# Attention and a two-layer expert in one planned kernel: the order of the first batch's units, a planner that counts instruction transfers, and one operation less per weight block

## The chip, the cores and the metric

The kernel runs on one core of one Trainium2 chip. The metric is the device time of one execution in microseconds (us). Before the change three runs gave 985.59, 986.07 and 987.94 us; the median is 986.07 us. The engines are PE (TensorE matmuls), PEld (its weight loads), DVE (VectorE), ACT (ScalarE), POOL (GpSimd) and SP (SyncE, which here only issues DMAs).

## The reference

Inputs are q, k and v (float32) of 8 batches, 8 heads, 576 positions and 64 channels, and the weights w_in (512 x 2048) and w_out (2048 x 512), which arrive as float64. The output is float32.

```
q_d, k_d, v_d = means of q, k, v over groups of 4 positions        # 144 positions
out_up  = repeat(softmax(q_d k_d^T / 8) v_d, 4)                     # each pooled row serves 4 positions
out_loc = softmax over |i - j| < 4 of (q k^T / 8), times v          # a band of 7 positions
x = (out_up + out_loc), heads side by side                          # 4608 tokens x 512
h = x @ w_in;  g = h * clip(h + 3, 0, 6) / 6
out = g @ w_out
```

## The kernel before, in words

**Tiling.** A unit is two heads of one batch on 128 partitions, so a batch has 4 units, named (batch, unit) below. A unit's work: load q, k and v, pool them by 4, pooled scores (L427) and banded scores (L605 puts the mask there, L613 multiplies), two softmaxes (L457 to L475), transposes of the probabilities (L482, L622), pooled products (L561), banded products (L633), and an addition into x (L663). For batch 0, q and k are transposed by PE (L279). Tokens are cut into chunks: 512, 256, then 384 each. For each chunk, x is split into a high part (L127 or L129) and a low part (L814), and then come, for 16 blocks of 128 hidden channels, the first expert product (L887, 12 matmuls), the gate (L894 relu on ACT, L898 on DVE), the gated value's high and low part (L902, L906) and the second expert product (L930, 3 matmuls for each 128 tokens).

**Weights.** They come as 64-bit words. For each of the 32 blocks (wi0 to wi15, wo0 to wo15) the kernel makes float32 bits from the two halves of a word: ACT rescales the high half (L180 into a PSUM bank for 5 early blocks, L184 in place for 27) and takes the top 3 bits of the low half (L195); DVE shifts the high half by 3 (L189), puts the sign in by an or (L191), and DVE or POOL adds the low bits (L199). ACT then writes the rounded part (L204) and DVE or POOL the rest (L208). A block that uses a PSUM bank holds it until its L208 is done; the banks are those that L930 writes (o0, o1, o2) or attention uses (a0 to a2).

**Order.** A planner (`Plan.emit`, L1177) simulates the five engines with costs written in the code, picks on each engine the ready operation whose latest time is smallest, and writes all instructions out in that order; each engine runs its own in that order. Latest times come from due times: `need(b)` less `unit_time` for each unit that follows in its batch. `UNIT_T` is 1.5 us for batch 0. `SLOTS` says which PSUM bank or piece of memory an operation may take.

**Unread products.** Where the plan sees a gap on PE before the first L887, `busy(n)` (L956) puts in n matmuls of 512 columns whose result nobody reads (L963), one for each 0.22 us of the gap less 0.1.

Of the kernel before, what the change touches and what calls it, by code (L numbers as in the profile page):

```python
# [64 lines left out]
def tile_local_down_attention_moe(ctx, tc, q_all, k_all, v_all, _qk_loc, _v_loc, w_in, w_out, ident_d, _mask_d, out):  # L65
# [7 lines left out]
    nc = tc.nc  # L73
# [89 lines left out]
    def plan_weight(n, kind, f, after, gate):  # L163
# [22 lines left out]
        def bits(i):  # L186
            z, high = zf_t[key].bitcast(I32), words["high"]
            if i == 0:
                nc.vector.tensor_scalar(z, z if by_bank else high, 3, None, op0=ALU.logical_shift_left)  # L189
            else:  # L190
                nc.vector.scalar_tensor_tensor(  # L191
                    out=z, in0=high, scalar=-0x80000000, in1=z, op0=ALU.bitwise_and, op1=ALU.bitwise_or)

        def low():
            nc.scalar.activation(words["low"], words["low"].bitcast(U32), AF.Copy, scale=2.0 ** -29)  # L195

        def add(eng):
            z = zf_t[key].bitcast(I32)
            eng.tensor_tensor(z, z, words["low"], op=ALU.add)  # L199

# [12 lines left out]
        c = op("ACT", 0.68, low, [ld])  # L213
        if by_bank:
            b = op("DVE", 0.75, partial(bits, 1), [op("DVE", 0.66, partial(bits, 0), [a])])
            d = op("DVE", 0.72, partial(add, nc.vector), [b, c])
        else:
            b = op("DVE", 0.75, partial(bits, 1), [op("DVE", 0.5, partial(bits, 0), [a])], lock=True)
            d = op(on("add", 1.0), 0, add, [b, c], lock=True)
        e = w_hi[key] = op("ACT", 0.6, hi, [d])  # L220
# [18 lines left out]
    def plan_duo(b, d, masked):  # L239
# [14 lines left out]
        if b < BY_PE:  # L254
            for kind, t in (("q", q_all), ("k", k_all)):
# [16 lines left out]
                for g in range(3):  # L272
# [14 lines left out]
                    l = pieces_[g if step == 3 else 0]  # L287
                    a = early_user(op("PE", 0.33, tr, [l], take=[(PS, key), ("qkd" + k0, hk)], free=[rk], lag=LAGT))
                    evicts[kind].append(op(
# [11 lines left out]
    def plan_unit(b, d, u, row0, k0, kv, PS, duo, evicts, users, masked, early_user, due):  # L301
# [377 lines left out]
        if alone:  # L679
            sd = early_user(op("PE", 0.9, scores_d, [pooled["q"], pooled["k"]], take=[bk, pk, sk], lag=LAGT))  # L680
        else:
            sd = sl_op = op(
                "PE", 1.5, scores_all,
                turned["q"] + turned["k"] + [pooled["q"], pooled["k"]] + masked,
                take=[bk, pk, sk] + bks + [pl, sl], lag=LAGT)
        sd_ops.append(sd)
# [22 lines left out]
        if alone:  # L709
            sl_op = early_user(op("PE", 1.3, scores_n, turned["q"] + turned["k"] + masked, take=bks + [pl, sl], lag=LAGT))  # L710
        s_ops.append(sl_op)
# [24 lines left out]
        if alone:  # L736
            evs_d = []
            for g in range(2):
                bk = (PS, ("td", un, g))
                t = early_user(op(  # L740
                    "PE", 0.3, partial(trans_d, g), [softmax_d], take=[tk_d, bk], free=[pk],
                    lag=LAGT))
                evs_d.append(op(on("ev", 6 * QB), 0, lambda eng, g=g: evict_d(eng, g), [t], free=[bk]))
            bk = (PS, ("od", un))
            a = early_user(op("PE", 0.64, pv_d, evs_d + sums, take=[bk, ok], free=[tk_d, ("vd" + k0, un)], lag=LAGT))
            od = early_user(op("ACT", 0.29, mean, [a], free=[bk]))
# [8 lines left out]
        if alone:  # L755
            a = early_user(op("PE", 1.5, pv_n, [t] + lv + ([od] if b else []), take=bks + xbs, free=[tk, vk], lag=LAGT))
        else:
            a = op("PE", 1.4, pv_all, [t] + lv + turned_d + sums, take=bks + [ok] + xbs,
                   free=[tk, vk, tk_d, ("vd" + k0, un)], lag=LAGT)
            od = op("ACT", 0.29, mean, [a], free=[bks[0]])  # L760
            od = op("DVE", 0.31, mean_too, [od], free=[bks[1]])
# [108 lines left out]
    def plan_moe(n):  # L870
# [6 lines left out]
        for f in range(NF):  # L877
# [26 lines left out]
            def lo(eng, st=st, key=key):  # L904
# [4 lines left out]
            a = op("PE", 2.11 * share, gemm1, split_done[n] + [w_done["i", f]] + ([last1] if last1 else []),  # L909
                   take=[("h", key)], dl=dl)  # L910
            last1 = a
# [9 lines left out]
        for f in range(NF):  # L921
# [16 lines left out]
            if f == 0 or f == NF - 1:  # L938
                ops_ = []
                for m in range(parts):  # L940
                    take = [(f"o{m}", n)] if f == 0 else []
                    ops_.append(op("PE", cost, partial(g, m), after + prev[-1:], take=take, dl=dl))
                    prev.append(ops_[-1])
            else:
                def all_parts(g=g):
                    for m in range(parts):
                        g(m)

                ops_ = [op("PE", cost * parts, all_parts, after + prev[-1:], dl=dl)]
                prev += ops_  # L950
# [50 lines left out]
T0, TC, TF, LAG = 55.0, 82.0, 5.1, 2  # L1001
UNIT_T, EARLY, SLACK = (1.5, 30.0, 30.0), 0.7, 28.0
PRE, GATE = 4, 8
# [19 lines left out]
COST = {  # L1023
    "add": {"POOL": (1.5, 0.0), "DVE": (0.68, 0.0)},
    "lo": {"POOL": (1.32, 0.0), "DVE": (0.68, 0.0)},
# [9 lines left out]
}  # L1035
PEN = {"add": {"DVE": 0.0}, "lo": {"DVE": 0.0}, "pool4": {"POOL": -10.0}, "ev": {"DVE": 5.0}, "sum4": {"POOL": -10.0},
    "norm": {"DVE": 5.0}, "minus": {"DVE": 5.0}, "xhi": {"DVE": 1.0}, "xlo": {"POOL": 2.0}, "gl": {"POOL": 10.0}, "ob": {"DVE": 5.0}}
# [98 lines left out]
def dma(packets, size):  # L1136

    return packets * (5.0 + 0.0376 * size) / 16e3 if size > 256 else packets * (8.0 + 0.039 * size) / 16e3


class Plan:
# [4 lines left out]

    def op(self, eng, cost, fn, after=(), take=(), free=(), size=0, dl=None, lag=0.0, lock=False):
        o = Op(len(self.ops), eng, cost, fn, take, size, dl)

        o.lag, o.lock = lag, {True: ("DVE", "POOL"), False: ("POOL",)}[lock]  # L1150
# [34 lines left out]
    def emit(self, warm, last, busy):  # L1185
# [41 lines left out]
        def fits(o):  # L1227
# [12 lines left out]
            return got  # L1240

        n_done = 0
        while n_done < len(self.ops):
            for e in ready:
# [22 lines left out]
                o.start = t  # L1267
                order.append(o)
                engine_free[e] = t + o.cost
# [37 lines left out]
        self.total = t  # L1307
        at = None
        for o in order:
            if o.eng == "PE" and at is not None:  # L1310
                n = int((o.start - at - IDLE[1]) / IDLE[0])
                if n > 0:
                    busy(n)
            if o is last:
                at, warm = None, None
            elif o.eng == "PE" and at is not None:
                at = o.end
            elif o is warm:
                at = o.end + 1.0
            o.run()  # L1320


class Op:
    def __init__(self, n, eng, cost, fn, take, size, dl):
# [5 lines left out]
        self.deps, self.succ, self.frees = [], [], []  # L1330
        self.at = 0.0
        self.span = self.cost + 2.0 + size
# [75 lines left out]
```

## Time and profile before

| what | value |
|---|---|
| median of three runs | 986.07 us |
| the profiled execution, its own time | 984.95 us |
| its span (first to last instruction) | 983.2 us |
| mean granted TensorE clock | 0.979 of full |
| first L887 starts | 65.90 us |
| PE, DVE busy share of the span | 97%, 59% |

The profiled execution's own time is 1.75 us above its span, and 1.12 us below the median of the runs. Shares over the span hide the stages: up to the first L887 PE runs attention of batch 0 while q, k, v and weights arrive; after that it alternates the two expert products with the attention units of later batches. The windows view below gives each engine's busy time by such stretches.

### The profile page before, as it was taken

To read this page: it belongs to the slowest core of one execution; us is meant where nothing else is said; L and a number is where in the kernel's file an instruction comes from. 1 tells how busy PE (TensorE), PEld (TensorE's weight loads), DVE (VectorE), ACT (ScalarE), POOL (GpSimd) and SP (SyncE) were. 2 spreads that over 40 slices of the span, in tenths; PEclk is the share of its full clock that TensorE was granted. 3 is DMA by queue.
4 is the path that set the end of the run, shared out by engine and by line. 5 is a ranking of instruction groups with operands and counts; after the bars stand their busy time and mean duration, and the time that the engine had idled before them with its cause. 6 is when DMAs were issued, how large, how long until landed. Compare 5 with 4: busy or idle time off the path is not lost.

```text
span 983.2 us, 21408 instructions
## 1 busy us (share of the span) xinstructions
PE 949.3 (97%) x8379; PEld 822.0 (84%) x8379; DVE 580.3 (59%) x1135; ACT 323.2 (33%) x641; POOL 342.7 (35%) x465
## 2 busy tenths in 40 slices
PE   6898999999999999999999999999999999999996
PEld 4576878798888888888898988888998988998995
DVE  6577999677656666666636557666635553323222
ACT  3356655333222322323322322322322322322221
POOL 5547674437434234334304343433404320000000
PEclk9778999999999999999999999999999999999999
DMA  8955543426665464563524455453523430100101
GB/s 195 246 163 154 162 133 110 97 60 141 123 130 108 108 114 95 109 121 77 113 48 86 103 109 101 106 116 76 122 52 75 102 70 3 33 1 1 33 1 33
DMA packets 318277, 94.16 MB, mean 96 GB/s; under 512 B 263680, under 2 KB 304512, under 8 KB 318176
## 3 DMA queue, kind: packets, MB, share of 16 engines
q1 hardware_dynamic: 318176, 92.79, 42.8%
q8 instruction: 66, 1.08, 0.5%
q14 instruction: 35, 0.29, 0.1%
HBM read 70.12 MB, written 22.61 MB: 94 GB/s over the span
## 4 chain that ended last, share of the span: by engine, by line
PE 68%; SPq 3%; DVE 2%; DMA 1%; issue 1%; POOL 0%; ACT 0%; DVEq 0%; POOLq 0%
PE o L930 32%; PE h L887 31%; PE a L646 2%; PE a L585 1%; PE a L443 1%; PE a L550 1%; SPq L528 1%; SPq L314 1%; SPq L502 1%; DMA arena<-in_q_dram 0%; SPq L507 0%; DMA arena<-pl 0%; DVE arena L321 0%; DMA out_dram<-arena 0%; DVE arena L330 0%
## 5 line engine op out<-in xcount | busy, mean ns | idle before, releaser
L887 PE MATMUL h<-rounded,wi 128*128 128x384 f32 (+2 forms) x2240 | 432.0, 336 | 2.0 <-DVE arena L898 1.8
L930 PE MATMUL o<-wo,rounded 128*128 128x512 f32 x1680 | 429.8, 397 | 2.9 <-DVE wi L208 2.8
L887 PEld LDWEIGHTS h<-rounded,wi 128*128 128x128 f32 x2240 | 389.5, 188 | 25.0 <-DVE arena L898 2.9
L930 PEld LDWEIGHTS o<-wo,rounded 128*128 128x128 f32 x1680 | 309.7, 188 | 64.6 <-DVE wi L208 3.0
L898 DVE SCALAR_TENSOR_TENSOR arena<-arena,h 128x384 f32<-128x384 f32 (+2 forms) x192 | 105.3, 549 | 197.8 <-ACT arena L894 197.0
L894 ACT ACTIVATE arena<-h 128x384 f32<-128x384 f32 (+2 forms) x192 | 94.3, 491 | 377.0 <-PE h L887 368.8
L902 ACT CAST rounded<-arena 128x384 fp32r<-128x384 f32 (+2 forms) x192 | 98.1, 512 | 139.3 <-DVE arena L898 93.3
L906 DVE TENSOR_TENSOR rounded<-arena,rounded 128x384 fp32r<-128x384 f32 (+2 forms) x135 | 80.2, 595 | 98.8 <-PE o L930 75.7
L906 POOL TENSOR_TENSOR rounded<-arena,rounded 128x384 fp32r<-128x384 f32 (+2 forms) x57 | 62.0, 1088 | 211.8 <-PE o L930 85.8
L460 POOL TENSOR_TENSOR arena<-arena 128x640 f32<-128x640 f32 x24 | 30.3, 1262 | 75.3 <-DVE arena L457 44.7
L475 POOL TENSOR_TENSOR arena<-arena 128x432 f32<-128x432 f32 (+2 forms) x47 | 51.1, 1095 | 9.1 <-DVE arena L472 7.6
L463 ACT ACTIVATE arena<-arena 128x432 f32<-128x432 f32 (+2 forms) x58 | 35.6, 630 | 49.4 <-DVE arena L460 44.7
L321 DVE STREAM_TRANSPOSE arena<-arena 128x576 f32<-128x576 f32 x56 | 42.6, 762 | 6.4 <-DMA arena<-in_q_dram 5.0
L466 DVE TENSOR_REDUCE arena<-arena 128x3 f32<-128x432 f32 (+2 forms) x58 | 37.9, 672 | 5.8 <-ACT arena L463 5.7
L814 POOL TENSOR_TENSOR rounded<-arena,rounded 128x768 fp32r<-128x768 f32 (+1 forms) x9 | 13.3, 1477 | 71.3 <-DVE rounded L129 70.2
L814 POOL TENSOR_TENSOR rounded<-first,rounded 128x384 fp32r<-128x384 f32 (+1 forms) x7 | 9.9, 1411 | 69.0 <-DVE rounded L129 69.0
L457 DVE TENSOR_REDUCE arena<-a 128x2 f32<-128x288 f32 (+3 forms) x59 | 22.8, 406 | 11.1 <-PE a L443 4.0
L336 POOL TENSOR_TENSOR arena<-arena 128x144 f32<-128x144 f32 x46 | 27.2, 591 | 3.6
L535 DVE STREAM_TRANSPOSE arena<-arena 128x640 f32<-128x640 f32 x24 | 20.0, 834 | 13.5 <-DMA arena<-pl 13.3
L334 POOL TENSOR_TENSOR arena<-arena 128x144 f32<-128x144 f32 x23 | 11.4, 498 | 46.1 <-DMA arena<-in_k_dram 18.1
L330 DVE TENSOR_REDUCE arena<-arena 128x144 f32<-128x576 f32 x35 | 25.8, 741 | 2.4 <-PE a L443 0.9
L646 PEld LDWEIGHTS a<-arena 64*64 64x64 f32 x960 | 16.4, 134 | 11.4 <-issue 8.3
(193 smaller groups left out, 862.3 us busy)
## 6 DMA issues: line engine op xcount, KB each, us to landing
rawi<-in_w_in_dram SPq DMA_DIRECT2D x16, 512.0 KB
rawo<-in_w_out_dram SPq DMA_DIRECT2D x16, 512.0 KB
arena<-in_q_dram SPq DMA_DIRECT2D x112, 72.0 KB
arena<-in_k_dram SPq DMA_DIRECT2D x112, 72.0 KB
pl<-arena SPq DMA_DIRECT2D x24, 320.0 KB
arena<-pl SPq DMA_DIRECT2D x96, 80.0 KB
out_dram<-arena SPq DMA_DIRECT2D x96, 72.0 KB
arena<-in_v_dram SPq DMA_DIRECT2D x24, 256.0 KB
```

What stands on the lines that cost most here:

```text
L321: nc.vector.transpose(out=qk[kind], in_=st["raw", kind].rearrange("p j i -> p (j i)"))
L460: eng.tensor_tensor(out_, x, m.unsqueeze(2).broadcast_to(list(x.shape)), op=ALU.subtract)
L463: nc.scalar.activation(x, x, AF.Exp, scale=scale)
L466: nc.vector.tensor_reduce(out=s, in_=x, op=ALU.add, axis=AX.X)
L475: eng.tensor_tensor(x, x, s.unsqueeze(2).broadcast_to(list(x.shape)), op=ALU.mult)
L646: nc.tensor.matmul(st["px"][g][h * D:(h + 1) * D, at + lo:at + hi], st["v"][ks, jj, h * D:(h + 1) * D], st["pt"][ks, jj, half + lo:half + ...
L887: nc.tensor.matmul(ps, win[f][:, wt, kk * P:(kk + 1) * P], xs[part][:, kk], start=(i == 0), stop=(i == 3 * NK - 1))
L894: nc.scalar.activation(st["t"], st["ps"], AF.Relu, bias=3.0)
L898: nc.vector.scalar_tensor_tensor(out=t, in0=t, scalar=6.0, in1=st["ps"], op0=ALU.min, op1=ALU.mult)
L902: nc.scalar.copy(st["gh"], st["t"])
L906: eng.tensor_tensor(st["gl"], st["t"], st["gh"].bitcast(F32), op=ALU.subtract)
L930: nc.tensor.matmul(otile[n, m], gt[:, ms], wout[f][:, wt], start=(f == 0 and i == 0), stop=(f == NF - 1 and i == 2),)
```

## The change

- The first DVE step of a weight block becomes one `scalar_tensor_tensor`: shift by 3, then an or with the low bits. The addition (L199) is gone. The ACT step that makes the low bits gets a bias of -0.5, so that its rounding gives whole numbers 0 to 7. The first DVE step now waits for both ACT steps.
- `UNIT_T` for batch 0 goes from 1.5 to 4.0 us, which spreads the four units' due times.
- Each PE operation tells the planner how many matmuls it issues (`rec`). The new `Plan.fetch` counts them in blocks of 128 (93 for the first) and adds time to an operation that would run into the next block sooner than 4.5 us after the block before it was entered.
- Unread products are planned for 0.75 of a gap (0.375 of it before plan time 8).
- The planner's cost of a DMA with packets of up to 256 bytes changes from (8 + 0.039 size) to (1 + 0.1 size) per 16,000 packets.

```diff
@@ bits, low, add (weight blocks) @@
             if i == 0:
-                nc.vector.tensor_scalar(z, z if by_bank else high, 3, None, op0=ALU.logical_shift_left)
+                nc.vector.scalar_tensor_tensor(
+                    out=z, in0=z if by_bank else high, scalar=3, in1=words["low"],
+                    op0=ALU.logical_shift_left, op1=ALU.bitwise_or)
...
-            nc.scalar.activation(words["low"], words["low"].bitcast(U32), AF.Copy, scale=2.0 ** -29)
-
-        def add(eng):
-            z = zf_t[key].bitcast(I32)
-            eng.tensor_tensor(z, z, words["low"], op=ALU.add)
+
+            nc.scalar.activation(words["low"], words["low"].bitcast(U32), AF.Copy, scale=2.0 ** -29, bias=-0.5)
...
+        b = op("DVE", 0.75, partial(bits, 0), [a, c], lock=not by_bank)
+        d = op("DVE", 0.75, partial(bits, 1), [b], lock=not by_bank)
...
-UNIT_T, EARLY, SLACK = (1.5, 30.0, 30.0), 0.7, 28.0
+UNIT_T, EARLY, SLACK = (4.0, 30.0, 30.0), 0.7, 28.0
...
-IDLE = 0.22, 0.1
+IDLE = 0.22, 0.1, 0.75
+
+FETCH = 128, 93, 4.5
...
+    def fetch(self, o):
+
+        t = o.start
+        if self.idle is None and self.warm.start is not None:
+            self.idle = self.warm.start + 1.2
+        if o is self.last:
+            self.last = None
+        if self.last is not None and self.idle is not None:
+            gap = (t - self.idle - IDLE[1]) * (IDLE[2] if t > 8.0 else 0.5 * IDLE[2])
+            o.busy = max(0, int(gap / IDLE[0]))
+        for n, first, took in ((o.busy, self.idle or 0.0, IDLE[0] * o.busy), (o.rec, t, o.cost)):
+            at, done = first, 0
+            while n - done >= self.left:
+                at += took * self.left / n
+                done += self.left
+                stall = max(0.0, self.block + FETCH[2] - at)
+                at += stall
+                if n is o.rec and first == t:
+                    o.cost += stall
+                self.block, self.left = at, FETCH[0]
+            self.left -= n - done
+        self.idle = t + o.cost
```

The instructions stand in another order on every engine. PE has 36 unread products before the first expert product where it had 63, and all else that it computes is the same. In the order's rows a name such as o0_597 is a tile in bank o0, "x48" counts matmuls as written, of which the chip runs L613, L427, L633 and L561 (L608, L422, L628 and L556 after the change, 5 lines earlier) as two each.

PE, between the second and the fourth unit of batch 0. Before, the last transposes of q and k (L279) come early, and three units' banded scores stand close together:

```order
L427 MATMUL o0_243<-early_160,arena_65 64x144 x6
L279 MATMUL o1_257<-ident_72,rows_64 128x128 x3
L279 MATMUL o2_263<-ident_72,rows_64 128x128 x3
L279 MATMUL h0_268<-ident_72,rows_64 128x128 x3
L427 MATMUL a0_273<-early_160,arena_65 64x144 x6
L605 LDWEIGHTS identb_74
L605 MATMUL a1_293<-maskn_75,identb_74 128x384
L613 MATMUL a1_293<-arena_65 32x32 x48
L605 LDWEIGHTS identb_74
L605 MATMUL o1_352<-maskn_75,identb_74 128x384
L613 MATMUL o1_352<-arena_65 32x32 x48
```

Now five transposes and six unread products stand between the second unit's banded scores and the third's:

```order
L422 MATMUL a2_235<-early_154,arena_65 64x144 x6
L600 LDWEIGHTS identb_74
L600 MATMUL o0_245<-maskn_75,identb_74 128x384
L608 MATMUL o0_245<-arena_65 32x32 x48
L274 MATMUL o1_309<-ident_72,rows_64 128x128 x3
L274 MATMUL o2_314<-ident_72,rows_64 128x128 x3
L274 MATMUL h0_325<-ident_72,rows_64 128x128 x3
L274 MATMUL a0_330<-ident_72,rows_64 128x128 x3
L274 MATMUL a1_335<-ident_72,rows_64 128x128 x3
```

What moved: the transposes of the second pair of units from ahead of the scores to between them. In the same way the first unit's products now stand ahead of the second unit's transposed probabilities, and the scores of unit (1,0) between the products of units (0,0) and (0,1); before, they stood after all products of batch 0, behind 6 and ahead of 11 unread products.

DVE, around the first expert products (L898 is the gate of one of them; wi4 is the fifth w_in block, which here lies in PSUM bank o0 until its L208). Before:

```order
L191 SCALAR_TENSOR_TENSOR o0_904<-rawi4_534,o0_904 128x512
L898 SCALAR_TENSOR_TENSOR arena_65<-arena_65,h0_1052 128x512
L199 ISA o0_904<-rawi4_534,o0_904 128x1024
L189 TENSOR_SCALAR early_139<-rawo2_1044 128x512
L129 COPY arena_65<-a0_1107 72x3x2x48
L898 SCALAR_TENSOR_TENSOR arena_65<-arena_65,h1_1080 128x512
L191 SCALAR_TENSOR_TENSOR early_132<-rawi3_514,early_132 128x512
L191 SCALAR_TENSOR_TENSOR early_132<-rawo1_518,early_132 128x512
L199 ISA early_132<-rawi3_514,early_132 128x1024
L622 STREAM_TRANSPOSE arena_65<-arena_65 128x384
L208 TENSOR_TENSOR wi4_1115<-o0_904,wi4_1115 128x512
```

Now bank o0 holds wi2, and this is what stands before the first gate (L893):

```order
L207 TENSOR_TENSOR wi2_980<-o0_654,wi2_980 128x512
L189 SCALAR_TENSOR_TENSOR early_146<-rawo0_510 128x512
L809 TENSOR_TENSOR lo_629<-arena_65,rounded_66 128x512
L461 TENSOR_REDUCE arena_65<-arena_65 128x12
L193 SCALAR_TENSOR_TENSOR early_146<-rawo0_510,early_146 128x512
L189 SCALAR_TENSOR_TENSOR early_215<-rawi3_528 128x512
L189 SCALAR_TENSOR_TENSOR early_215<-rawo1_599 128x512
L207 TENSOR_TENSOR wo0_1030<-early_146,wo0_1030 128x512
L193 SCALAR_TENSOR_TENSOR early_215<-rawi3_528,early_215 128x512
L893 SCALAR_TENSOR_TENSOR arena_65<-arena_65,h1_1013 128x512
```

What moved: the last use of bank o0 by a weight from behind the third gate to ahead of the first, and the last low part of x (L809) from POOL to DVE. On PE the first three second products of block 0 stood together after the third L887 group; now the first stands there, the second after the fourth group and the third after the fifth.

SP, which issues the loads. Before, two weight blocks go out ahead of the first q and k of batch 1; now they go out behind them:

```order
L349 DMA early_296<-in_v_dram 32x12x64 x4
L309 DMA arena_65<-in_q_dram 32x18x32 x4
L309 DMA arena_65<-in_k_dram 32x18x32 x4
L169 DMA rawi0_417<-in_w_in_dram 128x1024
L169 DMA rawi1_420<-in_w_in_dram 128x1024
L169 DMA rawi2_433<-in_w_in_dram 128x1024
L371 DMA arena_65<-in_v_dram 72x512 x2
```

What moved: the issue of the first two weight blocks goes past eight DMAs of q and k.

## Rows read from the trace of the kernel before

**Rows 1.** Windows by stage: stretch, length, busy (instructions) by engine, clock, DMA share, GB/s.
```profile
0.00:65.90 65.90, 52.38 (x1085) 36.18 (x1085) 38.26 (x90) 27.73 (x51) 32.44 (x58) 0.79 0.87 225
65.90:100.08 34.18, 30.75 (x323) 23.92 (x316) 29.12 (x53) 21.98 (x40) 26.28 (x26) 0.90 0.43 115
100.08:184.16 84.08, 80.94 (x836) 64.49 (x831) 78.70 (x130) 46.59 (x85) 52.77 (x52) 0.98 0.45 125
```

**Rows 2.** PE's waits: line, awaited, us in total, times, longest.
```profile
PE a L613 <- issue: 4.7, 1, 4.7
PE h L633 <- issue: 3.9, 1, 3.9
...
PE o L613 <- issue: 2.0, 1, 2.0
...
PE a L633 <- DVE arena L622: 1.4, 1, 1.4
```

**Rows 3.** Windows, PE alone: stretches between stalls, with busy time (matmuls), clock, DMA.
```profile
0.00:16.00 16.00, 13.02 (x221) 1.00 0.82 222
20.55:24.00 3.45, 2.53 (x128) 0.50 0.86 173
25.10:42.70 17.60, 17.53 (x378) 0.84 0.88 227
```

**Rows 4.** DMA view, 0 to 66 us: one instruction queue, packets, MB, share.
```profile
q8 instruction: 8, 0.13, 0.9%
```

**Rows 5.** Windows, all engines: three stretches at half clock.
```profile
20.50:30.70 10.20, 8.08 (x266) 6.54 (x267) 5.94 (x12) 1.65 (x3) 5.23 (x12) 0.50 0.87 213
44.40:61.40 17.00, 14.80 (x237) 10.66 (x236) 6.32 (x16) 8.50 (x19) 7.15 (x11) 0.50 0.99 234
78.50:85.30 6.80, 5.82 (x14) 4.55 (x15) 6.80 (x12) 4.00 (x7) 6.48 (x9) 0.50 0.40 83
```

**Rows 6.** Timeline of PE: start, us, engine, line, operation, out<-in, shapes, count.
```profile
11.18 1.02 PE L613 MATMUL a<-arena 64*32 64x32 f32 x96
...
30.46 6.11 PE L963 MATMUL h<-identb 128*128 128x512 bf16 x27
36.41 0.82 PE L482 MATMUL a<-ident,arena 128*72 128x128 f32 x6
...
39.69 1.60 PE L633 MATMUL a<-early,arena 32*64 32x28 f32 x96
...
49.53 2.78 PE L633 MATMUL a<-arena,early 32*64 32x28 f32 x96
...
61.42 0.95 PE L427 MATMUL a<-arena 64*64 64x144 f32 x12
...
79.48 4.21 PE L930 MATMUL o<-wo,rounded 128*128 128x512 f32 x9 [2.75 <-DVE wi L208]
...
105.65 2.20 PE L930 MATMUL o<-wo,rounded 128*128 128x512 f32 x9
```

**Rows 7.** Timeline of all engines around the end of batch 0's units.
```profile
58.75 2.74 PE L963 MATMUL h<-identb 128*128 128x512 bf16 x6
...
59.26 0.46 DVE L663 TENSOR_TENSOR arena<-a,early 128x288 f32<-128x288 f32 x1 [2.07 <-ACT early L566]
...
61.38 1.27 POOL L814 TENSOR_TENSOR lo<-arena,rounded 128x512 fp32r<-128x512 f32 x1 [2.85 <-ACT rounded L127]
```

**Rows 8.** Timeline of SP's issues.
```profile
25.59 0.95 SPq L169 DMA_DIRECT2D rawi<-in_w_in_dram  x2
26.66 3.45 SPq L314 DMA_DIRECT2D arena<-in_q_dram  x4
```

**Rows 9.** Weight steps by line: count, ns min/median/max, first to last start us.
```profile
L189 DVE TENSOR_SCALAR early<-rawi x8: 382/416/1518, 43.6 to 118.3; 128x512 int32<-128x512 int32 x8
...
L191 DVE SCALAR_TENSOR_TENSOR arena<-rawo,arena x8: 655/680/1314, 128.5 to 174.9; 128x512 int32<-128x512 int32 x8
...
L199 POOL TENSOR_TENSOR early<-early,rawo x6: 1315/1678/1760, 68.9 to 121.1; 128x512 int32<-128x512 int32 x6
```

More of the change, by code (lines that the diff above doesn't have):

```diff
@@ L287, in plan_duo @@
                     l = pieces_[g if step == 3 else 0]
-                    a = early_user(op("PE", 0.33, tr, [l], take=[(PS, key), ("qkd" + k0, hk)], free=[rk], lag=LAGT))
+                    a = early_user(op("PE", 0.33, tr, [l], take=[(PS, key), ("qkd" + k0, hk)], free=[rk], lag=LAGT, rec=3))
                     evicts[kind].append(op(
@@ L679, in plan_unit @@
         if alone:
-            sd = early_user(op("PE", 0.9, scores_d, [pooled["q"], pooled["k"]], take=[bk, pk, sk], lag=LAGT))
+            sd = early_user(op("PE", 0.9, scores_d, [pooled["q"], pooled["k"]], take=[bk, pk, sk], lag=LAGT, rec=12))
         else:
@@ L684, in plan_unit @@
                 turned["q"] + turned["k"] + [pooled["q"], pooled["k"]] + masked,
-                take=[bk, pk, sk] + bks + [pl, sl], lag=LAGT)
+                take=[bk, pk, sk] + bks + [pl, sl], lag=LAGT, rec=52)
         sd_ops.append(sd)
@@ L909, in plan_moe @@
             a = op("PE", 2.11 * share, gemm1, split_done[n] + [w_done["i", f]] + ([last1] if last1 else []),
-                   take=[("h", key)], dl=dl)
+                   take=[("h", key)], dl=dl, rec=12)
             last1 = a
@@ L941, in plan_moe @@
                     take = [(f"o{m}", n)] if f == 0 else []
-                    ops_.append(op("PE", cost, partial(g, m), after + prev[-1:], take=take, dl=dl))
+                    ops_.append(op("PE", cost, partial(g, m), after + prev[-1:], take=take, dl=dl, rec=3))
                     prev.append(ops_[-1])
@@ L947, in all_parts @@
                         g(m)
-                ops_ = [op("PE", cost * parts, all_parts, after + prev[-1:], dl=dl)]
+                ops_ = [op("PE", cost * parts, all_parts, after + prev[-1:], dl=dl, rec=3 * parts)]
                 prev += ops_
@@ L1023 @@
 COST = {
-    "add": {"POOL": (1.5, 0.0), "DVE": (0.68, 0.0)},
     "lo": {"POOL": (1.32, 0.0), "DVE": (0.68, 0.0)},
@@ L1035 @@
 }
-PEN = {"add": {"DVE": 0.0}, "lo": {"DVE": 0.0}, "pool4": {"POOL": -10.0}, "ev": {"DVE": 5.0}, "sum4": {"POOL": -10.0},
+PEN = {"lo": {"DVE": 0.0}, "pool4": {"POOL": -10.0}, "ev": {"DVE": 5.0}, "sum4": {"POOL": -10.0},
     "norm": {"DVE": 5.0}, "minus": {"DVE": 5.0}, "xhi": {"DVE": 1.0}, "xlo": {"POOL": 2.0}, "gl": {"POOL": 10.0}, "ob": {"DVE": 5.0}}
@@ L1136, in dma @@
 def dma(packets, size):
-    return packets * (5.0 + 0.0376 * size) / 16e3 if size > 256 else packets * (8.0 + 0.039 * size) / 16e3
+    return packets * (5.0 + 0.0376 * size) / 16e3 if size > 256 else packets * (1.0 + 0.1 * size) / 16e3
 class Plan:
@@ L1145, in __init__, with op @@
         self.ops, self.slots, self.slot = [], {}, {}
-    def op(self, eng, cost, fn, after=(), take=(), free=(), size=0, dl=None, lag=0.0, lock=False):
+    def op(self, eng, cost, fn, after=(), take=(), free=(), size=0, dl=None, lag=0.0, lock=False, rec=0):
         o = Op(len(self.ops), eng, cost, fn, take, size, dl)
+        o.rec = rec
         o.lag, o.lock = lag, {True: ("DVE", "POOL"), False: ("POOL",)}[lock]
@@ L1240, in fits @@
             return got
+        self.left, self.block, self.idle = FETCH[1], 0.0, None
+        self.warm, self.last = warm, last
         n_done = 0
@@ L1267, in emit @@
                 o.start = t
+                if e == "PE":
+                    self.fetch(o)
                 order.append(o)
@@ L1307, in emit @@
         self.total = t
-        at = None
         for o in order:
[L1310 to L1319, printed above, removed]
-            o.run()
+            if o.busy:
+                busy(o.busy)
+            o.run()
+    def fetch(self, o):
[19 more added lines that the diff above has]
+        self.idle = t + o.cost
 class Op:
@@ L1330, in __init__ @@
         self.deps, self.succ, self.frees = [], [], []
-        self.at = 0.0
+        self.at, self.start, self.busy = 0.0, None, 0
         self.span = self.cost + 2.0 + size
```

16 lines of the change are left out of this document (5 added, 11 removed).

## The prediction

> **What bounds the kernel now.** I read the windows by stage first [rows 1]: the reader is to see that PE is busy for 80.94 of 84.08 us from 100.08 to 184.16, but for 52.38 of 65.90 before the first L887 and 30.75 of 34.18 behind it. Later PE hardly waits, so the end comes as early as the first expert product starts and as PE then runs without a wait. Second, PE's waits [rows 2]: three of them, 10.6 us, are marked "issue", which is no engine and no DMA that the kernel issues. Third, what lies between those three [rows 3]: 221 matmuls, then 128, then 378, which is 384 less a few records. With their weight loads 128 matmuls are 256 instructions, and one queue carries instructions in 8 packets of 0.13 MB in all by 66 us [rows 4], about 256 instructions of 64 bytes a packet. So PE stands still where one packet ends and the next isn't there. From one such end to the next, 20.55 to 25.10, 4.55 us went by, of which PE worked 2.53. Fourth, the clock [rows 5]: 1.2 GHz (0.50) from 20.5 to 30.7 and from 44.4 to 61.4, each behind one of those stalls, and from 78.5 to 85.3 behind a 2.75 us wait [rows 6]. There 9 L930 take 4.21 us instead of 2.20, 96 L633 2.78 instead of 1.60. Last, the end of batch 0's units [rows 7].
>
> **The change part by part.** The sum is made against the profiled execution's 984.95 us (span 983.2); the median of the runs is 1.12 higher, which I add at the end.
>
> *First term: the start of the first L887, now 65.90 us.* I walk along PE's new order.
>
> (a) To the first stall. Its end, 20.55, goes by a packet and not by PE: PE now reaches the 221st matmul some 2 us sooner, at about 14, and waits longer. It counts 0. The seven unread products fewer at the very start lie ahead of loads that PE waits for; their cost, a later rise of the clock, is covered by the same stall.
>
> (b) From 20.55 to the end of the fourth unit's scores, now at 30.46 [rows 6]. The 2.0 us stall at the 349th matmul should go, because fifteen transposes and six unread products now lie between the ends of two packets; they cost 15 x 0.137 (0.82 for 6 L482) + 6 x 0.226 (6.11 for 27) = 3.4 us, double that at half clock, and 26 L613 lie ahead of the stall instead, 0.3. That is +1.1 to +4.5; two packets' ends bound it from below, 20.55 + 2 x 4.55 = 29.65, or -0.8. I take +1.0, nearest to the full clock, which six unread products on end should bring back.
>
> (c) From 30.46 to the last unit's products, now at 58.75 [rows 6, 7]. The 27 unread products there filled a wait for the first unit's softmax; with 5 more, 32 become 17: -15 x 0.226 = -3.4. The scores of unit (1,0) move in: 0.95 + 1.02 [rows 6] and a mask of some 0.3, +2.3. The 3.9 us stall goes; but two packets' ends now fall into the products of the last two units, which stand close: by 4.55 us a packet against some 3.5 us of work I put 1.0 each, +2.0. Sum -3.0.
>
> (d) From 58.75 to 65.90. Today 6 unread products, the scores of (1,0) and 11 more unread products lie here on PE, 7.15 us, though x's last low part ends at 61.38 + 1.27 = 62.65 [rows 7]. What stays is that chain alone: from the addition at 59.26 to 62.65 is 3.39, less 0.6 since DVE instead of POOL makes the last low part (0.68 for such an operation [rows 9]), plus 0.2 before and after it and 0.2 for the nine unread products and three transposes that fill it: 3.3. So -3.85. Late next is this chain itself.
>
> Together +1.0 - 3.0 - 3.85 = -5.85: the first L887 at 60.05 us. Bounds: at 2.4 GHz all the way, packets alone pace it, about 53; at 1.2 GHz all the way, 69 (worked out below).
>
> The Trainium skill's page "Runtime: NRT & Kernel Launch", section "Instruction fetch mechanics", speaks against this term: it says that instructions come in 16 KiB blocks of 256, and that the cost of going from one to the next is mostly hidden, since the sequencer hands them out more slowly than they arrive. The trace agrees on the blocks [rows 3, 4] and not on the hiding: 4.7, 2.0 and 3.9 us [rows 2]. By the page the stalls have another cause and stay, which is a rival below.
>
> *Second term: from the first L887 to 100.08.* PE idles 34.18 - 30.75 = 3.43 us there [rows 1], 2.75 of it ahead of the first L930 [rows 6], which needs bank o0; weight block wi4 held it until its last step, behind the third gate. Then 5.82 us of work run at half clock [rows 5], of which half, 2.9, is lost. In the new order bank o0 is freed ahead of the first gate, and the second L930 follows a fourth L887 group. What is late next is bank o1: from the first gate to the step that frees it DVE has 12 rows of about 0.6 us, 7.3; the gate can start some 3.6 us behind the first L887 (12 products of at most 0.244 and the relu), so it is free at 60.05 + 3.6 + 7.3 = 71. PE reaches it behind four L887 groups, one L930 triple, transposes and products of a unit, 4 x 2.9 + 0.7 + 1.0 = 13.3, at 73.4. That covers it by 2.4. So both losses go: -6.3 us (bounds -6.3 and, if one such wait stays, 0).
>
> *Weight steps.* On DVE 27 shifts grow from 0.42 to 0.68 by the nearest rows, L189 and L191 [rows 9] (+7.0), 22 additions of 0.68 go (-15.0), 8 last steps come over from POOL (+5.4): -2.6. POOL loses 10 additions of 1.68 and 8 steps of at least 1.3, 27 us. Nothing of it is on PE's path by itself; it buys DVE room in the stretch from 100.08, where DVE works 78.70 of 84.08 us [rows 1]. The fused operation isn't in the trace; it reads two strided SBUF streams, as L191 reads one. Bounds: 0.68 and L191's longest, 1.31; I take 0.68, its median. The first step's new wait for both ACT steps puts 0.7 ahead of it, hidden because the chain has room: the weights' issue moves from 25.59 behind eight q and k DMAs, four of which take 3.45 [rows 8], to about 34; 0.5 MB at 225 GB/s and five steps of 0.7 make 40 to 42, against a need at 60.
>
> The Trainium skill's "GPSIMD Engine Reference", section "Specifications", says that GpSimd's way to SBUF is shared with VectorE and that instructions with two SBUF inputs contend there; 27 operations change to such. Rows 9 show both: median 0.68, longest 1.31. By the page the first value is too low; the last rival below is that case.
>
> *Third term: from 100.08 to the end.* PE is 12.2 us ahead by then, and DVE, at 94%, must follow. Either the waits that rows 1 show there (3.1 us) go, or DVE gives back the lead beyond its 5.4 us of room. Between -3.1 and +4.2 I take one more wait of the kind in rows 2 (L633 for DVE), +1.4. The cheaper or dearer price of small DMA packets changes only when loads are issued; 0.
>
> Sum: 984.95 - 5.85 - 6.3 + 1.4 = 974.2, and with the 1.12 of the median 975.3 us.
>
> **The rivals.**
>
> *Packets alone pace the head.* If the clock stays at 2.4 GHz, the units' products shrink by the ratio 1.60 to 2.78 over most of 36.41 to 58.75 and the packets' ends bound it: the first L887 at about 53. Time 968. For it: six and ten unread products on end behind the stalls. Against it: from 44.4 PE worked 14.8 us before the clock rose at 61.4 [rows 5].
>
> *DVE gives the lead back.* If DVE at the point of 100.08 is no further than today, its 78.70 less 2.6 us pace what follows, up to 176.2 instead of 184.16: 8 us gained, 984.95 - 8.0 + 1.12 = 978.1. For it: 94%. Against it: DVE idles 27.6 of the first 65.9 us, and the head is what shortens.
>
> *Counting transfers does nothing* (the page's rule). The stalls of 2.0 and 3.9 stay and my 2.0 for two ends goes: 3.9 less gained, 979.2. Against it: the equal counts of rows 3.
>
> *Half clock throughout,* since fewer unread products run. About 5 us more for 36 to 42.5 us, which today runs at full clock, and 3.8 for 17 unread products: the first L887 at 69, 984.95 + 3.0 - 6.3 + 1.4 + 1.12 = 984.2, no change.
>
> *The fused step is slow, and DVE becomes the bound.* At 1.31 us instead of 0.68 for 27 blocks DVE has 17 us more between the first L887 and the next chunk: 29.12 + 78.70 - 2.6 + 17 = 122.2, from 60.05 to 182.3, so nearly all is gone (-1.9), and PE waits again and again with the clock falling, at 2.9 us each time as in rows 5, two times at least: 984.95 - 1.9 + 5.8 + 1.12 = 990. It decides from about 1.15 us per operation. Against it: L191 has two SBUF inputs for 27 blocks today, at a median of 0.68 [rows 9].
>
> **How the numbers follow.** The forecast (970 to 980) 0.50, packets alone 0.10, DVE gives back 0.13, transfers do nothing 0.12, half clock 0.08, slow fused step 0.07. Three runs tell 0.3% from no change, about 3 us: below 983.1 is faster, above 989 slower. The first four and no part of the last two are faster: 0.85; same 0.08; slower 0.07. The range leaves out the last two and half of the second: 967 to 983.
>
> **What would show it.** Right: the first L887 between 58 and 62 us; no "issue" wait at the third unit's scores; PE's waits marked "issue" some 8 us in all, the first of them near 6; no wait of L925 for a bank behind the third L882 group, and no half clock near 75 us; 64 weight steps of about 0.68 on DVE. Wrong: "issue" waits as long as before, a head past 64, DVE at 100% with PE waiting for it between 100 and 175, or fused steps over 1 us.

## The result, and the profile after

| | before | after |
|---|---|---|
| time, median (lowest to highest) | 985.83 us (983.41 to 987.94) | 977.0 us (976.4 to 978.71) |
| ratio after / before, 95% interval | | 0.9914 [0.9888, 0.994] |
| profiled execution, its span | 984.95 us, 983.2 | 976.4 us, 973.7 |
| first expert product (L887, now L882) | 65.90 us | 62.16 us |
| from there to the end of the span | 917.3 us | 911.5 us |

From the attention's lines on, line numbers are five lower than before (L887 is now L882); in the weight steps L191 has become L193, L195 L198, L204 L203 and L208 L207. The same three stages as in [rows 1], by windows: stretch, length, then busy time (instructions) of PE, weight load, DVE, ACT and POOL, clock, DMA share, GB/s.

```profile
0.00:62.16 62.16, 48.13 (x1060) 34.55 (x1061) 42.73 (x97) 29.69 (x55) 30.92 (x57) 0.87 0.95 209
62.16:89.86 27.70, 27.70 (x314) 21.94 (x312) 23.75 (x40) 21.81 (x40) 12.98 (x18) 0.98 0.80 202
89.86:172.60 82.74, 79.89 (x833) 63.35 (x826) 72.32 (x119) 46.36 (x84) 37.83 (x43) 0.98 0.45 131
```

The head (all that stands ahead of the first expert product) is 3.7 us shorter and the stretch behind it 6.5; in that stretch PE is now busy without a break. The third is 1.3 shorter. PE's waits, against [rows 2] (line, awaited, us in total, times, longest):

```profile
PE h L958 <- DVE arena L141: 2.9, 1, 2.9
PE a L641 <- DMA arena<-in_v_dram: 2.7, 1, 2.7
PE a L477 <- POOL arena L470: 2.4, 2, 1.6
PE a L600 <- ACT early L127: 2.4, 1, 2.4
PE o L925 <- DVE wo L207: 2.0, 1, 2.0
PE o L608 <- ACT arena L127: 1.7, 1, 1.7
PE h L477 <- POOL early L470: 1.3, 1, 1.3
PE o L925 <- DVE rounded L901: 1.1, 1, 1.1
PE h L628 <- issue: 0.9, 1, 0.9
...
PE o L628 <- issue: 0.3, 1, 0.3
```

The 10.6 us of "issue" are 1.2 now. What came in their place in the head are waits for ACT's copies (L127: 2.4 and 1.7 us) and POOL's scaling (L470: 1.6 and 1.3), which a late PE didn't meet before; the L641 and L925 rows lie behind the first expert product, and the 2.9 us are the wait for the first data, which before has too. The end of batch 0's units, against [rows 7] (start, us, engine, line, operation, tiles, shapes, count):

```profile
57.84 0.46 DVE L658 TENSOR_TENSOR arena<-a,early 128x288 f32<-128x288 f32 x1 [1.85 <-PE a L628]
57.85 4.02 PE L958 MATMUL h<-identb 128*128 128x512 bf16 x9
...
59.99 0.60 ACT L127 CAST rounded<-arena 128x512 fp32r<-128x512 f32 x1
...
60.62 0.69 DVE L809 TENSOR_TENSOR lo<-arena,rounded 128x512 fp32r<-128x512 f32 x1 [0.70 <-ACT rounded L127]
...
61.66 0.84 PE L477 MATMUL a<-ident,arena 128*72 128x128 f32 x3
62.16 0.77 PE L882 MATMUL h<-rounded,wi 128*128 128x512 f32 x1
```

The clock, against [rows 5], by windows: two stretches at 0.50 in the head; the one near 80 us is gone.

```profile
42.50:49.35 6.85, 6.85 (x175) 6.05 (x162) 4.72 (x12) 4.49 (x10) 1.97 (x3) 0.50 1.16 232
...
52.80:63.00 10.20, 9.89 (x123) 6.25 (x119) 7.08 (x17) 5.38 (x11) 3.99 (x4) 0.50 0.85 225
```

The weight steps. First before, by windows of one line over the whole span: L189 (shift), L191 (sign) on DVE; L199 (addition) and L208 (low part) on DVE, then POOL.

```profile
0.00:983.20 983.20, 20.16 (x32) 0.98 0.43 96
0.00:983.20 983.20, 23.99 (x32) 0.98 0.43 96
0.00:983.20 983.20, 16.44 (x22) 14.96 (x10) 0.98 0.43 96
0.00:983.20 983.20, 9.89 (x13) 24.94 (x19) 0.98 0.43 96
```

After: L189 (fused shift and or), L193 (sign), L207 (low part, DVE and POOL).

```profile
0.00:973.70 973.70, 23.91 (x32) 0.99 0.44 97
0.00:973.70 973.70, 21.21 (x32) 0.99 0.44 97
0.00:973.70 973.70, 16.41 (x21) 15.26 (x11) 0.99 0.44 97
```

On DVE they fell from 70.5 to 61.5 us, on POOL from 39.9 to 15.3. One fused step, by the view of its line (ns shortest/median/longest, first and last start; it answers to [rows 9]):

```profile
L189 DVE SCALAR_TENSOR_TENSOR early<-rawi x8: 678/685/1346, 48.8 to 130.8; 128x512 int32<-128x512 int32 x8
```

POOL is rid of its 10 additions, and 8 low parts went from it to DVE. By the profile alone all this reads as the prediction has it: a shorter head, a wait for a bank gone, a little given back. The experiments say something else.

### The profile page after: what moved, and what is told of

Its sections match the earlier page's. It is cut to its first block, busy times and chain, and to the rows that moved or that the text cites. A ratio compares the mean times of both kernels' runs of the same rounds, so it can differ in the third digit from the quotient of the medians.

```text
span 973.7 us, 21275 instructions
## 1 busy us (share of the span) xinstructions
PE 943.7 (97%) x8352; PEld 820.0 (84%) x8352; DVE 589.9 (61%) x1147; ACT 325.2 (33%) x645; POOL 295.3 (30%) x423
## 4 chain that ended last, share of the span: by engine, by line
PE 84%; SPq 5%; DVE 4%; DMA 3%; issue 1%; POOL 1%; ACT 1%; DVEq 0%; ACTq 0%; POOLq 0%
PE h L882 38%; PE o L925 36%; PE a L641 2%; SPq L309 1%; PE a L580 1%; PE a L438 1%; PE a L545 1%; PE a L925 1%; DMA early<-in_v_dram 1%; DMA arena<-pl 1%; DMA rawi<-in_w_in_dram 1%; SPq L502 1%; SPq L523 1%; PE a L628 1%; SPq L497 1%
## 5 line engine op out<-in xcount | busy, mean ns | idle before, releaser
L882 PE MATMUL h<-rounded,wi 128*128 128x384 f32 (+2 forms) x2240 | 433.4, 337 | 0.2 <-POOL rounded L809 0.2
L925 PE MATMUL o<-wo,rounded 128*128 128x512 f32 x1680 | 429.3, 397 | 3.0 <-DVE wo L207 2.0
L882 PEld LDWEIGHTS h<-rounded,wi 128*128 128x128 f32 x2240 | 390.6, 189 | 22.3 <-issue 1.8
L925 PEld LDWEIGHTS o<-wo,rounded 128*128 128x128 f32 x1680 | 309.2, 188 | 64.4 <-issue 3.6
L893 DVE SCALAR_TENSOR_TENSOR arena<-arena,h 128x384 f32<-128x384 f32 (+2 forms) x192 | 105.3, 549 | 190.1 <-ACT arena L889 189.5
L901 POOL TENSOR_TENSOR rounded<-arena,rounded 128x384 fp32r<-128x384 f32 (+2 forms) x51 | 53.6, 1052 | 200.1 <-PE o L925 118.6
L470 POOL TENSOR_TENSOR arena<-arena 128x432 f32<-128x432 f32 (+2 forms) x44 | 46.0, 1058 | 3.0 <-ACT wi L203 1.6
L329 POOL TENSOR_TENSOR arena<-arena 128x144 f32<-128x144 f32 x29 | 13.7, 472 | 82.9 <-DVE arena L316 43.4
L809 POOL TENSOR_TENSOR rounded<-arena,rounded 128x768 fp32r<-128x768 f32 (+2 forms) x8 | 11.7, 1468 | 75.0 <-DVE rounded L129 73.9
L331 POOL TENSOR_TENSOR arena<-arena 128x144 f32<-128x144 f32 x58 | 33.0, 568 | 4.5
L387 DVE TENSOR_REDUCE arena<-arena 128x128 f32<-128x512 f32 (+2 forms) x28 | 29.6, 1059 | 3.9 <-PE a L545 2.1
L641 PEld LDWEIGHTS a<-arena 64*64 64x64 f32 x960 | 16.7, 134 | 12.2 <-issue 6.0
L882 PE MATMUL h<-lo,wi 128*128 128x512 f32 x64 | 25.1, 393 | 0.0
```

Of the source, the lines that this page charges most:

```text
L331: eng.tensor_tensor(t, t, x[:, :, r], op=ALU.add)
L470: eng.tensor_tensor(x, x, s.unsqueeze(2).broadcast_to(list(x.shape)), op=ALU.mult)
L641: nc.tensor.matmul(st["px"][g][h * D:(h + 1) * D, at + lo:at + hi], st["v"][ks, jj, h * D:(h + 1) * D], st["pt"][ks, jj, half + lo:half + ...
L882: nc.tensor.matmul(ps, win[f][:, wt, kk * P:(kk + 1) * P], xs[part][:, kk], start=(i == 0), stop=(i == 3 * NK - 1))
L893: nc.vector.scalar_tensor_tensor(out=t, in0=t, scalar=6.0, in1=st["ps"], op0=ALU.min, op1=ALU.mult)
L901: eng.tensor_tensor(st["gl"], st["t"], st["gh"].bitcast(F32), op=ALU.subtract)
```

## The experiments

Theory A was that of the prediction: the planner's rules (units in turn, transfers counted, fewer unread products) carry the gain, and the weight steps only make room. Ratios are to before, run beside each, with 95% intervals. "Own order" means that only what is issued changes and each instruction stays in its place; otherwise the planner orders everything anew.

### The two halves of the change

**Weight steps as before, all the planner's rules new (e7).**

```diff
-                nc.vector.scalar_tensor_tensor(
-                    out=z, in0=z if by_bank else high, scalar=3, in1=words["low"],
-                    op0=ALU.logical_shift_left, op1=ALU.bitwise_or)
+                nc.vector.tensor_scalar(z, z if by_bank else high, 3, None, op0=ALU.logical_shift_left)
...
+            eng.tensor_tensor(z, z, words["low"], op=ALU.add)
```

> The changed kernel with the weight steps of before (shift, add on VectorE or GpSimd), everything else as changed; the order is planned anew. Rival B (the weight steps are worth some 4 us in any order, as their splitting was in the changed order): 980 to 983. Theory A (the planner finds room for them): 976 to 979.

980.49 us, 0.9978 [0.9956, 0.9999]: rival B.

**The fused weight step, all the planner's rules old (e8).** The same edit the other way, in the kernel before.

> The kernel before with the fused weight step alone; the order is planned anew with the old costs. Theory A: 981 to 985, head within 1.5 us of 65.9, since without the additions the old order gained 1.7 us of 984.3. Rival B (the weight steps alone carry most of the gain): 976 to 979.

975.32 us, 0.9919 [0.989, 0.9949]: rival B, and below its range.

| ratio to before | rules old | rules new |
|---|---|---|
| weight steps old | 1 | 0.9978 [0.9956, 0.9999] |
| fused step | 0.9919 [0.989, 0.9949] | 0.9914 [0.9888, 0.994] |

The fused step alone gives what the whole change gives; the rules alone give about 2 us, and on top of the fused step nothing that can be measured. e8 has its units in the old order and its waits for instructions (2.9 and 3.5 us), and still its last products run at full clock and the first expert product starts earlier than in the changed kernel. Its timeline (a view from 50 us on, which leaves out the first of the five unread products at 49.2):

```profile
49.64 1.56 PE L958 MATMUL h<-identb 128*128 128x512 bf16 x4
...
54.60 1.60 PE L628 MATMUL a<-early 32*64 32x28 f32 x96
...
60.08 0.50 PE L882 MATMUL h<-rounded,wi 128*128 128x512 f32 x1
```

### What of the weight step it is

**After, own order, fused step taken apart (e2).**

```diff
-                nc.vector.scalar_tensor_tensor(
-                    out=z, in0=z if by_bank else high, scalar=3, in1=words["low"],
-                    op0=ALU.logical_shift_left, op1=ALU.bitwise_or)
+                nc.vector.tensor_scalar(z, z if by_bank else high, 3, None, op0=ALU.logical_shift_left)
+                nc.vector.tensor_tensor(z, z, words["low"], op=ALU.bitwise_or)
```

> The changed kernel, in its own order, with the fused shift-and-or taken apart again into a shift (0.42 us) and an or of two SBUF inputs (0.68 us): 32 more instructions on VectorE, 0.42 us each or 13.4 us in all. Theory A: 977 to 980, since VectorE waits for PE later on. Theory B: at least 983.

981.19 us, 0.9963 [0.995, 0.9976], 4 to 5 us more than the changed kernel (977.0; its variants e3 and e4, run beside e2, took 976.25 and 976.65): over A's range, under B's.

**e8, own order, the same edit (e9).**

> The kernel of e8 (before with the fused weight step, order planned anew), in its own order, with the fused step taken apart into a shift (0.42 us) and an or (0.68 us): 32 more instructions, 13.4 us, on VectorE, none on GpSimd. Theory E (the weight steps carry the gain by their own time on VectorE): 979 to 982, as in e2 over the changed kernel. Theory F (they carry it by the order that the planner finds without the additions, and by GpSimd being rid of 11 of them): 975 to 977.5.

981.28 us, 0.9985 [0.9971, 0.9999], some 6 us more than e8: theory E. Windows from the first expert product over the same PE work, e8 first, then e9:

```profile
60.08:118.80 58.72, 55.11 (x516) 43.81 (x517) 49.45 (x82) 39.36 (x73) 28.70 (x31) 0.94 0.63 189
118.80:186.80 68.00, 66.10 (x704) 53.37 (x703) 54.89 (x91) 36.30 (x70) 28.97 (x32) 1.00 0.41 111
```

```profile
58.45:118.50 60.05, 53.52 (x515) 42.52 (x516) 56.20 (x99) 39.58 (x73) 27.15 (x31) 0.97 0.63 189
118.50:189.20 70.70, 67.54 (x704) 54.39 (x704) 60.83 (x105) 36.30 (x71) 28.55 (x32) 0.98 0.40 107
```

DVE works 12.7 us more, and PE stands still for 6.53 + 3.16 us instead of 3.61 + 1.90: 4.2 more. PE's longest waits in e9's stretch are 3.5 us for DVE (L616, the transposed probabilities) and 2.7 for ACT's rounded weights; in e8's they are 1.7 and 1.9. The same for the changed kernel and e2:

```profile
62.16:113.80 51.64, 51.64 (x515) 41.34 (x514) 45.89 (x78) 37.79 (x69) 21.40 (x27) 0.99 0.76 208
113.80:183.80 70.00, 67.16 (x703) 54.40 (x702) 55.40 (x93) 34.48 (x66) 29.41 (x33) 0.98 0.37 100
```

```profile
67.22:119.40 52.18, 51.43 (x514) 41.17 (x513) 51.15 (x88) 36.00 (x67) 22.16 (x27) 1.00 0.61 158
119.40:191.80 72.40, 67.94 (x704) 54.34 (x703) 63.93 (x110) 35.38 (x67) 29.19 (x33) 0.98 0.39 107
```

DVE works 13.8 us more and PE's idle time goes from 2.84 to 5.21. So a third to a sixth of DVE's added time in this stretch comes out as time of PE, in waits on several lines. In e2's profiled run another 5.1 us lie ahead of the first expert product; how much of that is chance one trace can't tell. Both runs keep an order that was planned for the fused step; planned for the split one, it might cost less.

That time put on DVE costs PE doesn't yet say that e8 gains by time taken off DVE. These are the same two stretches in the kernel before:

```profile
65.90:124.00 58.10, 54.67 (x523) 43.33 (x517) 52.05 (x90) 37.53 (x68) 42.56 (x42) 0.94 0.49 135
124.00:194.10 70.10, 66.96 (x703) 54.50 (x702) 58.98 (x100) 34.29 (x64) 37.23 (x37) 0.98 0.44 113
```

In e8 DVE works 6.7 us less here and POOL 22.1 less, but the two stretches take 126.72 us instead of 128.20: only 1.5 of the 9.1 us between the two profiled runs. Another 1.8 come later, and 5.8 lie in the head: the last unit's products end at 56.1 instead of 58.75, with the clock back at 50.7 instead of 61.4, and behind them 7 unread products stand on PE instead of 17. By these traces the greater part of e8's gain is thus in the order that the planner found anew, ahead of the first expert product.

**Before, own order, no additions (e1), and without GpSimd's alone (e10).** By the trace they are 22 on DVE and 10 on POOL.

```diff
         def add(eng):
-            eng.tensor_tensor(z, z, words["low"], op=ALU.add)
+            pass                        # e1;  e10: "if eng is nc.vector:" ahead of it
```

> The kernel before, in its own order, without the 32 additions of the weights' low bits (21 on VectorE at 0.68 us, 11 on GpSimd at 1.68 us; their low bits are left out of the weights). Theory A (the order carries the gain; the weight steps only make room): 984 us, between 982 and 987, with the first expert product within 0.5 us of 65.9 and the wait ahead of the first L930 shorter by no more than 2. Theory B (VectorE's room is the gain): 977 to 980, and the 2.75 us wait for bank o0 gone.

> The kernel before, in its own order, without the 11 additions on GpSimd alone (their low bits are left out of the weights); the 21 on VectorE stay. Theory F: as e1, 1.5 to 2.5 us under before, and from the first expert product to the end 912 to 914 us instead of 917.3. Theory E: within 0.7 us of before, 916 to 918 us behind the first expert product.

e1: 982.63 us, 0.9985 [0.9973, 0.9997], first expert product at 66.13, bank o0 still awaited for 2.2 us: theory A's numbers. e10: 983.76 us, 1.0007 [0.9998, 1.0015], from the first expert product to the end 916.3 us: in that order POOL's additions are worth nothing measurable, so e1's gain is DVE's. But in the order that was planned with additions, taking them out brings 1.7 us, not 8. The rest needs the new order. Whether the planner finds it by the room on DVE or by that on POOL is open: no run planned the order anew without POOL's additions alone.

### The planner's rules one by one

**Units as before (e5), transfers not counted (e6), in the changed kernel; units in turn in e8 (e12).**

```diff
-UNIT_T, EARLY, SLACK = (4.0, 30.0, 30.0), 0.7, 28.0
+UNIT_T, EARLY, SLACK = (1.5, 30.0, 30.0), 0.7, 28.0    # e5; e12 the other way, in e8
-FETCH = 128, 93, 4.5
+FETCH = 128, 93, 0.0                                   # e6
```

> The changed kernel with the first number of UNIT_T at its old 1.5 (due times of batch 0's units 1.5 us apart instead of 4.0), everything else as changed; the order is planned anew, and the scores of the second, third and fourth unit stand close together again, as before. Theory A (the units in turn shorten the head): first expert product at 64 to 67 us, a wait for instructions of 2 us or more in the scores, 979 to 983 us. Rival (what is done with units doesn't matter; banks and weight steps carry the gain): 975.5 to 978.

> The changed kernel with FETCH's 4.5 us at 0, so that the planner counts no instruction transfers; the order is planned anew. Its first 330 matmuls on TensorE are almost the changed kernel's; later the scores of unit (1,0) go behind the third unit's products. Theory A (counting transfers moves work to where PE would stand still): first expert product at 63 to 66, 978 to 981 us. Rival (counting transfers does nothing, since the packets land at times that the planner doesn't know): 975.5 to 978.

> The kernel of e8 with the units in turn as well (UNIT_T 4.0), order planned anew, without the count of transfers, the share of unread products and the new DMA price. If units in turn help on top of the fused step: under 974. If the order of the units is worth nothing by itself, as e5 against the changed kernel says: 974.5 to 977.5. If each new plan falls within some 2 us of chance: either, and e8 stays the best.

e5: 976.84 us, 0.9936 [0.9915, 0.9958], first expert product at 59.4 with 2.5 and 3.2 us of waits for instructions: the rival. e6: 979.41 us, 0.9959 [0.9937, 0.9981], first expert product at 65.3: A's numbers, though its interval overlaps the changed kernel's. e12: 977.0 us, 0.9949 [0.9931, 0.9968]. The order of the units is worth nothing measurable by itself; e8 stays the best, level with the changed kernel. The share of unread products and the price of small DMAs were tried only together with the other rules (e7). The five plans with the fused step spread over 4 us, from 975.3 to 979.4, whatever rule is changed; the two without it, before and e7, lie above them (980.5 and more). So the gain isn't one lucky plan, though the intervals of e6 and e7 overlap, and a difference of 2 us between two plans can be chance.

### Unread products and the clock

**After, own order, no unread products behind the first four (e3), and eight more ahead of unit (1,0)'s scores (e4).**

```diff
-            if o.busy:
+            if o.busy and o.start < 8.0:          # e3
+            if o.busy or more:                    # e4: more = 8 ahead of the fifth scores_n, else 0
```

> The changed kernel, in its own order, without the 32 unread products (L958) behind the first four. Theory A (they hold TensorE's clock up, and lie in waits): half clock from about 20 us on through the whole head, first expert product at 64 to 67 us instead of 62.2, 979 to 982 us. Rival C (they cost as much as they give: the nine behind the last unit's products run 4.0 us at half clock): first expert product at 60 to 62, 975 to 977.

> The changed kernel, in its own order, with eight more unread products in the 2.35 us wait ahead of the scores of unit (1,0) (39.4 to 41.7 us), behind which the clock fell at 42.5. Theory A (the half clock from 42.5 to 49.4 and from 52.8 to 63.0 costs PE's time in the head): the clock stays at 1.00 at least to 50, first expert product 1.5 to 3.5 us earlier than 62.2, 973.5 to 975.5 us. Rival D (the head is paced by the chain of the units through VectorE, ScalarE and GpSimd and by the packets): first expert product within 0.7 us of 62.2, 976.5 to 977.5.

e3: 976.25 us, 0.9921 [0.9893, 0.9949]; it runs at half clock from 24.3 to 41.3 and from 48.1 to 65.2 us, its first expert product starts at 62.90, between the two theories, and the time is the same: rival C's. e4: 976.65 us, 0.9932 [0.9911, 0.9954]: rival D in time. Its clock did stay at 1.00 from 26.1 to 53.4, as theory A had it; PE stood still for instructions there, 1.3 us at 46.1 and 3.4 at 53.6. But its profile shows more: up to 41 us its instructions on PE are the changed kernel's, one by one, and yet its second unit's scores stood still.

```profile
13.89 0.84 PE L608 MATMUL o<-arena 64*32 64x32 f32 x74
21.50 0.54 PE L608 MATMUL o<-arena 64*32 64x32 f32 x22 [6.76 <-issue]
```

The same scores in the changed kernel:

```profile
15.99 1.02 PE L608 MATMUL o<-arena 64*32 64x32 f32 x96
```

By the records of the instruction queue its first packet started at 18.7 us in e4 and at 13.3 in the changed kernel. e4's first expert product came at 65.89, and its profiled run took 979.51 us against its median of 976.65. That these 2.9 us are this packet's chance is likely and not shown: of the five runs another took 979.56, without a trace.

**Before, own order, five more unread products (e11).**

```diff
+            if turned == 7 and not more:          # ahead of the fourth unit's transposes
+                more = True
+                busy(5)
```

> The kernel before, in its own order, with five more unread products ahead of the fourth unit's transposes (52.2 us), where e8 had four ahead of its own at 49.6 us and its clock rose at 50.7. Theory G (the head's start goes by the clock in the last two units' products): the clock rises by 54 instead of 61.4, first expert product at 62 to 64, 1.5 to 3.5 us under before. Rival D (the chain through the units and the packets sets it): first expert product within 0.7 of 65.9, the time within 0.7 us of before.

982.48 us, 0.9993 [0.9972, 1.0013]; twelve runs from 977.45 to 988.58. The profiled run is the fastest of them. Its windows show what was expected, the clock back at 53.4 us, and its first expert product came at 62.14:

```profile
39.70:53.40 13.70, 12.01 (x217) 9.21 (x217) 5.92 (x14) 6.07 (x14) 5.84 (x9) 0.50 1.02 250
53.40:62.10 8.70, 8.70 (x239) 5.56 (x238) 6.80 (x15) 7.01 (x14) 4.29 (x4) 1.00 0.82 256
```

The median didn't move. By the profile it is theory G, by the median rival D. The other eleven runs left no trace, but each run's mean granted clock is on record: the five runs at 0.982 or more took 977.45 to 981.29 us, the seven at 0.981 or less 982.28 to 988.58. So this kernel's time goes with its clock, and it seems that five products more don't bring it back in every run; what decides in which is open. One thing more: behind its first expert product e11 issues what before issues, and needs 913.6 us from there where before's trace has 917.3. A single trace can be off by that much.

## Why the prediction was right, and where it was not

The time, 975.3 forecast and 977.0 measured, is within its range, and that is in good part luck: two terms of the head came out with the other sign, and the sum holds nothing for the half of the change that gives the gain. Of the signs that were named, three came (no "issue" wait at the third unit's scores, no wait for a bank behind the third group nor half clock near 75, fused steps of about 0.68 us at the median); the first product at 62.16 is just outside 58 to 62, and of some 8 us of "issue" there were 1.2.

- **The head, -5.85 forecast, -3.74 measured.** (a) and (b), +1.0 forecast, came to -3.2: the fourth unit's scores end at 27.29 us, not 30.46. Before, PE went on at 20.6 behind a packet that started at 17.7 us; but in the changed kernel's trace that packet started at 13.3, and PE, which reached the 221st matmul at 16.6 and not at 14, went on at once. (c), -3.0 forecast, came to +2.3: PE now met waits for POOL (1.6 and 1.3 us), DVE (0.7) and ACT (2.4), which the walk along PE's order didn't have, and ran at half clock from 42.5 to 49.4 and from 52.8 on. (d), -3.85 forecast, came to -2.8. Its sum has a slip: the stretch begins at 58.75, but the chain in its place is counted from 59.26, so 0.5 us is missing. And the 3.3 us from the addition to the first product were 4.32, since the last low part began 2.78 behind the addition instead of 2.12 [rows 7], and since nine unread products, counted with little, ran at half clock until 61.87, 0.56 behind the low part that the first product needs.
- **The 2.0 and 3.9 us stalls** went, as forecast, and it matters little: e5 and e8 keep such stalls and start their expert products at 59.4 and 60.1. In the changed kernel's trace the waits for POOL, DVE and ACT took up what PE saved.
- **Bank o0, -6.3 forecast, -6.5 measured** in its stretch. But the gain doesn't need it: e8 has no wait for the bank and yet, over the same work, idles 3.61 us where before idles 3.43, at the same clock of 0.94, and is the fastest of all. Nor is the half clock there fixed: it lasted 6.8 us in before's trace and 3.5 in e11's, which issues the same from there on.
- **Given back, +1.4 forecast, +0.7 measured** (10.2 us ahead at 89.86, 9.5 at the end), but not where it was put: in the stretch that starts there, with DVE at 87%, PE gained another 1.3 us, and the 2.1 were lost behind 172.60.
- **The step that failed: "Nothing of it is on PE's path by itself", of the weight steps.** They were given -2.6 us on DVE and no share in the sum. On DVE they came to -9.0: the prediction took 0.42 us for the old shift, the shortest rows' median [rows 9], where the mean over 32 is 0.63, so that fusing cost 3.8 us and not 7.0; the additions took 16.4 and not 15.0; and the sign steps became 2.8 cheaper, which wasn't counted. And they are on PE's path: put back as 32 more DVE instructions they cost some 4 to 6 us (e2, e9), and they are the half of the change that gives the gain (e8 against e7). The rival "DVE gives the lead back" had a part of the mechanism, that DVE's time behind the first expert product costs PE; by e1 and by e8's windows that part is worth about 1.5 us. The rest of the 8 comes by the order planned anew, by e8's trace in the head; why the fused step lets the planner find such an order stays open.
- **The slow fused step** is refused: its median is 0.685 us, its mean 0.75, its longest 1.35. The Trainium skill's "GPSIMD Engine Reference", section "Specifications", has GpSimd share VectorE's way to SBUF, with contention when an instruction has two SBUF inputs; the few long ones would fit that, but no run here shows GpSimd to be what held them.
- **That the cost of instruction fetch is mostly hidden** (the Trainium skill, "Runtime: NRT & Kernel Launch", "Instruction fetch mechanics"): the 6.76 us in e4 disagree with it as [rows 2] do. That counting transfers in the plan is worth something rests on e6 alone, 2.4 us by the medians with overlapping intervals; that stays open.

## What to carry to other kernels

A profile whose stages move as forecast doesn't show which part of the change moved them: run each half alone before you say so. An engine at 83% beside a TensorE at 96 to 98% isn't free: 13 to 14 us more on VectorE made TensorE stand still for 2.4 and 4.2 us more. Work taken off it paid 1.7 us in the old order and 8 with the order made anew, so plan again when you save on an engine that isn't the busiest. Cost an instruction by its mean over all its forms, and look at where the medians of several runs stand before you read a few microseconds out of one trace.

## What the runs showed of the hardware

The first packet of the instruction queue started between 13.3 and 18.7 us in fourteen profiled runs, by the trace's records of that queue. Where PE passed its 94th matmul at 11.6 us (before and e4), the packet started 6.1 and 7.1 us later; where it passed it at 11.8 to 14.5 us (the other twelve), 0.8 to 3.1 us later. So the PE that was earliest at this point was the one that stood still longest. DMA was at 0.82 of its time or more in that stretch [rows 3]; that this load holds the packet up was not tried.
